# Reordering the start of a four-layer spectral kernel: x and C first, the branch later, TensorE on zeros meanwhile

## The chip, the cores and the metric
The kernel runs on one core of one Trainium2 chip. The metric is device time in microseconds (us): 1197.44 is the median of three runs (1197.13 to 1198.53). A core has TensorE (PE in the profile; PEld are its weight loads), VectorE (DVE), ScalarE (ACT), GpSimd (POOL) and SyncE (SP), which here only issues DMAs. Each engine works its own queue of instructions in order, and semaphores order the engines among each other.

## The reference, cut to what matters
Two kinds of layer alternate, A, B, A, B, on x of 2048 positions by 576 channels; each adds its result to x. The inputs of B (k, v, both kernels) are the same in both B layers.

```python
x = A_x                                        # 2048 x 576
x = x + _A_ref(_layernorm(x), dft_seq_re, dft_seq_im, dft_hid_re, dft_hid_im)
x = x + _B_ref(_layernorm(x), B_k, B_v, B_shift_k, B_ssm_k, B_ssm_D)
x = x + _A_ref(_layernorm(x), ...)             # layer 3
x = x + _B_ref(_layernorm(x), ...)             # layer 4
# _A_ref: a = x @ hid_re.T, b = x @ hid_im.T; y = seq_re @ a - seq_im @ b
# _B_ref: kv = shift_conv(k) * v; y = q * (long_conv(kv, ssm_k) + kv * ssm_D), q the normed x
```

## The kernel before
All products are in fp32r, a rounded fp32. To keep accuracy, an operand is split into a rounded part (a copy by ScalarE) and a remainder (a subtraction by VectorE); a product of two split operands takes three matmuls. `split` (L94 to L96) does this: L95 is the copy, L96 the subtraction.

**Layer 1** (`layer`, L297) multiplies the sequence matrix C with the normed x first and the hidden matrix afterwards. It goes through blocks of 512 output positions (`tb`), both matrices (`g`) and 16 rows of x (`k`, also called j); one combination is a *step*. A step is 14 matmuls: 12 on the four accumulators s (for each of four column blocks x high by C high, x high by C remainder, x remainder by C high) and 2 on rm, for the last 64 channels. Steps are counted from 0; steps 0 to 15 bring the 16 rows of x in, later steps use them again.

What a step needs: its C tile, loaded two steps ahead into the ring `craw` and split into one of three places of the ring `cs` (`load_c`); and its x row. `get_x0` (L688) loads row j+2, makes the statistics of row j and j+1 (`stats0`), scales row j and splits it (`to_x`, L190: rounding at L192, remainders at L194 and L195). For the first eight rows (ASTAT) VectorE makes the statistics (`norm_stats`, L178 to L180: 2 + 1 + 1 instructions), GpSimd the power -1/2 (L181), VectorE the bias (L187), ScalarE the scaling (L188). For the others ScalarE sums and squares (L646, L648), with one-column instructions by VectorE between (L647, L649, L672), and scales (L673). `layer` asks for rows up to XLEAD = 3 ahead.

**The branch** (`branch`, L346) computes what layer B needs of k, v and the long kernel. Its first stage, called F1 here, is a generator: each `next(br)` runs one piece. It loads rows of ssm_k (L415) and v, convolves k on VectorE (L390, L395), multiplies with v (L423), splits (L95, L96) and makes groups of six small products (`f1_products`) into banks bk, which ScalarE copies out (L448) and stores. The first piece starts the generator, which also adds a third place to `craw`. The convolution is spread over the pieces from the third feed on. The variable `used` counts pieces; after each half step the main loop runs pieces until `want`, 5 a 8 steps up to step 16, then faster, till step 42. After that follow the middle of the branch (`mid`, L509 to L531) and the hidden products of layer 1 (`hidden`, bk<-w,u), also drawn piece by piece.

**Banks.** PSUM has eight banks: four s, one rm, and three for everything else. `bank()` hands out the three in fixed turns.

**Order.** A scheduler puts the instructions of each engine into one queue, by its own estimates; `behind(i)` and `issue_after(i)` add an edge: what is issued inside stands behind i on its engine's queue. No engine waits for another by such an edge, but what stands behind a waiting instruction waits too.

**The start before**: the loading of x row 0, the first branch piece, row 0 of x, then a second piece, C of steps 0 and 1, x rows 1 and 2, two pieces, row 1, two pieces; then the steps, with `used` = 4.

Of the kernel before, what the change touches and what calls it, by code (L numbers as in the profile page):

```python
# [10 lines left out]
F32 = mybir.dt.float32  # L11
# [4 lines left out]
P = 128  # L16
# [15 lines left out]
F1_16 = 5  # L32
VW = 384
F1_END = 42
W_FROM = 41
# [30 lines left out]
def fnet_h3_kernel(ctx: ExitStack, tc: tile.TileContext, x, c_mat, w_re, w_im, k_pad, v, shift_k,  # L66
# [9 lines left out]

    banks, given = [psp.tile([P, NT], F32, tag=f"b{i}", name=f"bk{i}") for i in range(3)], [0]

    def bank():
        given[0] += 1  # L80
        return banks[(given[0] - 1) % 3]

# [77 lines left out]

    scaled = []

# [11 lines left out]
    def norm_stats(src):  # L174
        m = ring["stat"]()
        st, mv, ve, rs = m[:, :12].rearrange("p (a c) -> p a c", a=2), m[:, 12:14], m[:, 14:15], m[:, 15:16]
        for i in range(2):
            nc.vector.bn_stats(st[:, i, :], src[:, i * HD:(i + 1) * HD])  # L178
        nc.vector.bn_aggr(mv, st)
        nc.vector.tensor_scalar(ve, mv[:, 1:2], EPS, None, op0=OP.add)  # L180
        pows.append(nc.gpsimd.tensor_tensor(rs, ve, mhalf, OP.pow).ins)  # L181
        return mv, rs, m[:, 16:17]
# [26 lines left out]

    def load_c(step):  # L210
        g, tb, k = step
        raw = ring["craw"]()
        anchor.append(load_after(raw, c_mat[g, tb, k]) if anchor else nc.sync.dma_start(raw, c_mat[g, tb, k]).ins)
        c = ring["cs"]()
# [131 lines left out]
    def branch():  # L346
# [91 lines left out]
        def f1_products(j, fc, xf, at, n, so, to):  # L438
            ps = [bank()[:, :n] for _ in range(2)]
            last = seq[-1:]  # L440
            for k, (a, b) in enumerate(((0, 1), (0, 0), (1, 0))):
                for i in (1, 0):
                    half = slice(i * HP, (i + 1) * HP)
                    with behind(*last):
                        last = [mm(ps[i], fc[half, a, :], xf[b][half, at:at + n], k == 0, k == 2)]
            so = two(ring[so]())
            for i in range(2):
                stored[:] = [nc.scalar.activation(so[:, i, :], ps[i], AF.Copy).ins]  # L448
            nc.scalar.dma_start(t_d[:, j::J, to:to + n], so)
# [224 lines left out]

    XL, LN = {}, {}

    def load_x(j):
        if j < J:
            XL[j] = ring["x"]()
            nc.sync.dma_start(XL[j], x[:, j, :])  # L680

# [6 lines left out]
    def get_x0(j):  # L688
        if X[j] is None:
            if j > 0:  # L690
                load_x(j + 2)
            stats0(j)
            if j > 0:
                with behind(*stored):
                    stats0(j + 1)
# [36 lines left out]
    def done1(j, xa):  # L732
# [423 lines left out]
```

## Time and profile before
| What | us |
|---|---|
| median of three runs | 1197.44 |
| the profiled execution, its own time | 1199.58 |
| span of the profiled execution | 1197.8 |
| TensorE busy in the span | 1175.3 |
| VectorE busy | 839.2 |
| ScalarE busy | 660.5 |
| TensorE busy, first 4 us / next 4 us | 0.00 / 1.21 |
| TensorE busy, 8 to 12 us | 3.30 |
| VectorE busy, 50 to 60 us / 60 to 70 us | 8.27 / 9.56 |

Busy time counts an engine's instructions, overlaps once. The span runs from the first to the last instruction; 1.8 us of the execution lie around it. The timeline prints when an instruction or a run of equal ones started, in us from the span's start, how long it took, and in brackets how long its engine had been idle and what released it. Tiles are named output<-inputs: early and flts hold raw data, mats the split x and C, f1f and f1r the branch's rows and their split parts.

### The profile page before, as it was taken

How to read it: one execution, taken by the hardware profiler on the slowest of the kernel's cores; microseconds unless marked ns; L12 is line 12 of the kernel's file. 1: busy time of each engine (PE TensorE's matmuls, PEld its weight loads, DVE VectorE, ACT ScalarE, POOL GpSimd, SP SyncE). 2: the span in 40 equal slices, each digit the busy share in tenths (PEclk: the TensorE clock that was granted, in tenths of full speed). 3: DMA queues.
4: the chain of work that ended last, by engine and by line, in shares of the span. 5: the costliest groups of instructions: out<-in, count | busy, mean ns of one | idle time of the engine just before them, and what ended most of it. 6: DMA issues, size and time to landing. Idle time of an engine off the chain costs nothing.

```text
span 1197.8 us, 18057 instructions
## 1 busy us (share of the span) xinstructions
PE 1175.3 (98%) x6248; PEld 996.6 (83%) x6248; DVE 839.2 (70%) x1498; ACT 660.5 (55%) x1311; POOL 75.1 (6%) x116
## 2 busy tenths in 40 slices
PE   7999999999999999999999999999999999999997
PEld 5776667888888888888988898888888888789997
DVE  7899983679777677675347766865776777774764
ACT  7865555669877668775435666634444445450210
POOL 2210000000000000001101121000000000001111
PEclk9999999999999999999999999999999999999999
DMA  9869898446656667648957676872772787795621
GB/s 337 294 196 315 260 300 268 158 133 182 221 189 199 212 174 209 199 138 270 289 200 237 222 256 216 272 259 71 224 277 71 218 278 257 242 317 173 218 88 41
DMA packets 142845, 259.84 MB, mean 217 GB/s; under 512 B 15649, under 2 KB 43553, under 8 KB 142754
## 3 DMA queue, kind: packets, MB, share of 16 engines
q1 hardware_dynamic: 102674, 205.45, 52.9%
q10 hardware_dynamic: 33168, 42.63, 10.2%
q0 software_dynamic: 6912, 10.62, 3.5%
q8 instruction: 49, 0.80, 0.3%
q14 instruction: 42, 0.34, 0.1%
HBM read 191.99 MB, written 66.65 MB: 216 GB/s over the span
## 4 chain that ended last, share of the span: by engine, by line
PE 76%; ACT 2%; DVE 2%; DMA 1%; issue 1%; POOLq 0%; DVEq 0%; ACTq 0%
PE s L75 42%; PE bk L75 30%; PE rm L75 4%; ACT flts L509 1%; DMA flts<-in_c_mat 0%; ACT u L95 0%; ACT mid L509 0%; DVE u L96 0%; DVE mid L515 0%; DVE flts L529 0%; ACT mats L95 0%; DVE flts L530 0%; DMA xa<-flts 0%; DMA mid<-td 0%; DVE flts L528 0%
## 5 line engine op out<-in xcount | busy, mean ns | idle before, releaser
L75 PE MATMUL s<-mats 128*128 128x512 f32 x2088 | 541.2, 395 | 1.5 <-ACT mats L192 0.9
L75 PEld LDWEIGHTS s<-mats 128*128 128x128 f32 x2088 | 381.4, 188 | 84.1 <-issue 10.9
L96 DVE TENSOR_TENSOR mats<-flts,mats 128x512 fp32r<-128x512 f32 x206 | 140.7, 687 | 64.3 <-ACT mats L95 63.8
L95 ACT ACTIVATE mats<-flts 128x512 fp32r<-128x512 f32 x206 | 128.5, 628 | 85.4 <-PE bk L75 28.4
L75 PE MATMUL bk<-mid 128*128 128x288 f32 x768 | 135.5, 301 | 3.0 <-ACT flts L509 1.6
L75 PEld LDWEIGHTS bk<-mid 128*128 128x128 f32 x768 | 116.9, 188 | 24.1 <-ACT flts L509 7.0
L75 PE MATMUL bk<-w,u 128*128 128x288 f32 x864 | 120.6, 295 | 0.9 <-ACT w L237 0.5
L75 PEld LDWEIGHTS bk<-w,u 128*128 128x128 f32 x864 | 117.8, 188 | 3.5 <-ACT w L237 0.8
L515 DVE TENSOR_TENSOR mid<-flts,mid 128x576 fp32r<-128x576 f32 (+1 forms) x149 | 93.4, 628 | 34.3 <-ACT mid L509 30.5
L509 ACT ACTIVATE flts<-bk 128x288 f32<-128x288 f32 x160 | 62.2, 404 | 88.8 <-PE bk L75 82.4
L75 PE MATMUL rm<-mats 128*128 128x512 f32 x304 | 95.1, 391 | 0.0
L509 ACT ACTIVATE flts<-flts 64x288 f32<-64x288 f32 x192 | 85.0, 443 | 5.5
L509 ACT ACTIVATE mid<-flts 128x576 fp32r<-128x576 f32 (+1 forms) x148 | 80.4, 575 | 7.2 <-DMA flts<-td 3.1
L284 DVE TENSOR_TENSOR flts<-flts,bk 128x288 f32<-128x288 f32 x48 | 21.7, 453 | 69.9 <-PE bk L75 69.9
L448 ACT ACTIVATE flts<-bk 128x384 f32<-128x384 f32 (+1 forms) x104 | 43.1, 462 | 45.7 <-PE bk L75 45.6
L75 PE MATMUL bk<-mats 128*128 128x288 f32 (+1 forms) x376 | 67.8, 317 | 0.0
L75 PEld LDWEIGHTS rm<-mats 128*128 128x128 f32 x304 | 57.1, 188 | 12.1 <-issue 0.2
L75 PE MATMUL s<-t,mats 128*128 128x512 f32 x264 | 65.0, 390 | 0.0
L181 POOL TENSOR_TENSOR flts<-flts 128x1 f32<-128x1 f32 x35 | 28.7, 820 | 523.1 <-DVE flts L180 523.0
L75 PE MATMUL bk<-mats,t 128*128 128x288 f32 (+1 forms) x368 | 59.3, 303 | 0.0
L75 PEld LDWEIGHTS bk<-mats 128*128 128x128 f32 x376 | 55.6, 188 | 3.4
L75 PEld LDWEIGHTS s<-t,mats 128*128 128x128 f32 x264 | 49.4, 188 | 10.6 <-DVE t L96 0.4
(145 smaller groups left out, 1465.3 us busy)
## 6 DMA issues: line engine op xcount, KB each, us to landing
flts<-in_c_mat SPq DMA_DIRECT2D x148, 256.0 KB, 3.5
ph<-in_c_mat SPq DMA_DIRECT2D x54, 512.0 KB, 4.7
flts<-in_c_mat SPq DMA_DIRECT2D x30, 512.0 KB, 5.0
flts<-td SPq DMA_DIRECT2D x53, 288.0 KB, 3.1
td<-flts ACTq DMA_DIRECT2D x36, 384.0 KB, 4.6
vd<-flts ACTq DMA_DIRECT2D x64, 144.0 KB, 2.4
flts<-vd SPq DMA_DIRECT2D x32, 288.0 KB, 4.6
mid<-in_i2c POOLq DMA_DIRECT2D x32, 256.0 KB, 4.9
```

The source lines that it names most:

```text
L75: return nc.tensor.matmul(ps, lhsT, rhs, start=first, stop=last, skip_group_check=more).ins
L95: a = nc.scalar.activation(h, src, AF.Copy).ins
L96: return a, nc.vector.tensor_tensor(l, src, h.bitcast(F32), OP.subtract).ins
L181: pows.append(nc.gpsimd.tensor_tensor(rs, ve, mhalf, OP.pow).ins)
L284: added[:] = [nc.vector.tensor_tensor(r[:, cs], r[:, cs], ps[:, :HD], OP.add).ins]
L448: stored[:] = [nc.scalar.activation(so[:, i, :], ps[i], AF.Copy).ins]
L509: last_act.append(nc.scalar.activation(*args, **kw).ins)
L515: nc.vector.tensor_tensor(l, src, h.bitcast(F32), OP.subtract)
```

## The change
- The branch no longer runs at the start: `used` starts at -2, `want` is at - 2 up to step 16 (one piece a step) and as before from 16 on. Its first piece, and with it the third place of `craw`, comes in step 1. Its constants f1c all come through GpSimd's queue, since the powers are then already in the list.
- SP's queue starts with x row 0, C of step 0, x row 1, C of step 1, x row 2.
- The main code splits C of step 0 itself, its remainder behind the statistics of row 1, and runs the statistics one row ahead: row 1's behind the bias of row 0, row 2's behind C of step 1.
- `warm()` sets 512 columns of the last x row to zero and makes 18 products of them into a bank, before the first real product on TensorE's queue.
- Later x loads stand behind the last C load; the branch's pieces get further edges, behind the rounding of an x row and the last loads.
- `f1_products` and the zeros use three fixed banks in turns (`turn`); `bank()` takes a tile from the pool (tag b, three places) each time.

```diff
+WARM = 18
+    def turn():
+        given[0] += 1
+        return banks[(given[0] - 1) % 3]
     def bank():
-        given[0] += 1
-        return banks[(given[0] - 1) % 3]
+        return psp.tile([P, NT], F32, tag="b", bufs=3, name="bk")
...
         def f1_products(j, fc, xf, at, n, so, to):
-            ps = [bank()[:, :n] for _ in range(2)]
+            ps = [turn()[:, :n] for _ in range(2)]
...
             if j > 0:
-                load_x(j + 2)
+                with behind(anchor[-1]):
+                    load_x(j + 2)
             stats0(j)
             if j > 0:
-                with behind(*stored):
+                with behind(*stored, made[j - 1]):
                     stats0(j + 1)
...
+    def warm():
+        t = xs[:, J - 1, :NT]
+        nc.vector.memset(t.bitcast(F32), 0.0)
+        b = turn()
+        for i in range(WARM):
+            mm(b, t[:, :P], t, i == 0, i == WARM - 1)
...
     load_x(0)
-    next(br)
-    get_x0(0)
-    with tc.issue_after(biased[0]):
-        next(br)
-        with behind(*parted, scaled[0]):
-            load_c((0, 0, 0))
-        load_x(1)
-        with behind(rounded[0]):
-            load_c((0, 0, 1))
-        load_x(2)
-    used = 4
-    first_lo = parted[1]
-    next(br)
-    next(br)
-    with behind(first_lo):
-        get_x0(1)
-    next(br)
-    next(br)
+    raws = []
+    for i in range(2):
+        with behind(loaded[-1]):
+            raws.append(raw_step((0, 0, i)))
+        with behind(anchor[-1]):
+            load_x(i + 1)
+    warm()
+    stats0(0)
+    first = ring["cs"]()
+    CT[0, 0, 0] = first[:, :NT], first[:, NT:]
+    nc.scalar.activation(first[:, :NT], raws[0], AF.Copy)
+    next(LN[0][1], 0)
+    with behind(biased[0]):
+        stats0(1)
+    with behind(varied[1]):
+        low = nc.vector.tensor_tensor(first[:, NT:], raws[0], first[:, :NT].bitcast(F32), OP.subtract).ins
+        X[0] = to_x(LN[0][0], 0)
+    with behind(made[0]):
+        next(LN[1][1], 0)
+    with behind(biased[1], rounded[0]):
+        load_c((0, 0, 1), raws[1])
+    with behind(halved[1]):
+        stats0(2)
+    used = -2
...
-            want = int(4 + F1_16 * at / 8 if at <= 16 else at16 + (68 - at16) * (at - 16) / (F1_END - 16))
-            with behind(made[min(n + 2, J - 1)], *evac):
+            want = int((16 + 2 * F1_16 - 10) * at / 16 - 2 if at <= 16 else at16 + (68 - at16) * (at - 16) / (F1_END - 16))
+            with behind(made[min(n + 2, J - 1)], *evac, *rounded[min(n, 4) + 1:min(n, 4) + 2],
+                        *(loaded[-1:] + anchor[-1:] if n < J else [])):
```

More of the change, by code (lines that the diff above doesn't have):

```diff
@@ L75, in mm, with bank @@
         return nc.tensor.matmul(ps, lhsT, rhs, start=first, stop=last, skip_group_check=more).ins
-    banks, given = [psp.tile([P, NT], F32, tag=f"b{i}", name=f"bk{i}") for i in range(3)], [0]
-    def bank():
+    banks, given = [psp.tile([P, NT], F32, tag=f"b{i}", name=f"bf{i}") for i in range(3)], [0]
+    def turn():
         given[0] += 1
         return banks[(given[0] - 1) % 3]
+    def bank():
+        return psp.tile([P, NT], F32, tag="b", bufs=3, name="bk")
     acc4 = [psp.tile([P, NT], F32, tag=f"s{i}", name=f"s{i}") for i in range(4)]
@@ L159, in fnet_h3_kernel @@
     anchor, made, rounded, pows, biased, halved, added, evac, parted, stored = [], [], [], [], [], [], [], [], [], []
-    scaled = []
+    scaled, varied = [], []
     def load_after(dst, src):
@@ L179, in norm_stats @@
         nc.vector.bn_aggr(mv, st)
-        nc.vector.tensor_scalar(ve, mv[:, 1:2], EPS, None, op0=OP.add)
+        varied.append(nc.vector.tensor_scalar(ve, mv[:, 1:2], EPS, None, op0=OP.add).ins)
         pows.append(nc.gpsimd.tensor_tensor(rs, ve, mhalf, OP.pow).ins)
@@ L208, in fnet_h3_kernel, with raw_step @@
     CT = {}
-    def load_c(step):
+    def raw_step(step):
         g, tb, k = step
@@ L213, in load_c @@
         anchor.append(load_after(raw, c_mat[g, tb, k]) if anchor else nc.sync.dma_start(raw, c_mat[g, tb, k]).ins)
+        return raw
+    def load_c(step, raw=None):
+        raw = raw_step(step) if raw is None else raw
         c = ring["cs"]()
@@ L673, in normed_x @@
         nc.scalar.activation(y, src, AF.Identity, bias=nb, scale=rs)
-    XL, LN = {}, {}
+    XL, LN, loaded = {}, {}, []
     def load_x(j):
@@ L679, in load_x @@
             XL[j] = ring["x"]()
-            nc.sync.dma_start(XL[j], x[:, j, :])
+            loaded.append(nc.sync.dma_start(XL[j], x[:, j, :]).ins)
     def stats0(j):
```

## Prediction
> **What bounds the kernel now.** I read the busy line of the page first, then the windows, then the timeline of the first 100 us engine by engine. In the windows the columns are the stretch, its length, and the busy time of each engine with its number of instructions; then clock, DMA share, GB/s.
>
> ```profile
> PE 1175.3 (98%) x6248; PEld 996.6 (83%) x6248; DVE 839.2 (70%) x1498; ACT 660.5 (55%) x1311; POOL 75.1 (6%) x116
> ...
> 12.00:16.00 4.00, 4.00 (x11) 3.09 (x11) 4.00 (x17) 3.17 (x6) 2.17 (x4) 1.00 1.03 375
> ...
> 80.00:90.00 10.00, 9.82 (x52) 7.12 (x51) 10.00 (x12) 5.45 (x13) 1.05 (x2) 1.00 0.83 247
> ...
> 70.00:1180.00 1110.00, 1103.46 (x5898) 939.94 (x5897) 774.97 (x1347) 604.26 (x1199) 55.59 (x89) 1.00 0.67 215
> ```
>
> TensorE is busy 98% of the span; from 70 to 1180 us it idles 6.5 us (1110 - 1103.46). So over the whole kernel TensorE sets the time, and idle time at its start is lost. But between 80 and 90 us VectorE has not a tenth free either: there two engines bound one stage, and that decides this change.
>
> The start of the kernel now (start, length, engine, line, operation, tiles, count, idle time before):
>
> ```profile
> 0.81 0.06 DVE L171 MEMSET flts<- 128x1 f32 x1 [0.81 <-PEq L1148]
> ...
> 3.69 0.82 DVE L178 BATCH_NORM_STATS2 flts<-early 128x6 f32<-128x288 f32 x2 [2.82 <-DMA early<-in_x]
> ...
> 5.86 0.87 ACT L188 ACTIVATE early<-early,flts 128x576 f32<-128x576 f32 x1 [0.27 <-DVE flts L187]
> ...
> 6.64 1.09 PE L75 MATMUL bk<-f1r 64*128 64x288 f32 x6 [6.64 <-DVE f1r L96]
> ...
> 7.15 0.67 ACT L192 ACTIVATE mats<-early 128x576 fp32r<-128x576 f32 x1
> ...
> 7.88 1.56 PE L75 MATMUL s<-mats 128*128 128x512 f32 x2 [0.15 <-ACT mats L192]
> ...
> 10.14 1.09 PE L75 MATMUL bk<-f1r 64*128 64x288 f32 x6 [0.70 <-ACT flts L448]
> ...
> 11.15 4.56 PE L75 MATMUL s<-mats 128*128 128x512 f32 x10
> ...
> 15.55 0.63 PE L75 MATMUL rm<-mats 128*128 128x512 f32 x2
> ...
> 18.77 0.62 PE L75 MATMUL rm<-mats 128*128 128x512 f32 x2
> ...
> 21.95 0.61 PE L75 MATMUL rm<-mats 128*128 128x512 f32 x2
> ...
> 25.98 0.62 PE L75 MATMUL rm<-mats 128*128 128x512 f32 x2
> ```
>
> A step of layer 1 is 14 products and ends with the two on rm. The ends stand at 15.55, 18.77, 21.95: a step costs 3.18 us, 0.227 a product. From 21.95 to 25.98 one branch group (six products) lies between: it costs 0.85. The ten products from 11.15 to 15.55 take 0.44 each, twice as long, though the window from 12 to 16 shows a granted clock of 1.00: TensorE is slow until about 15.4. Step 1 thus begins at 16.0, with one step and two branch groups done.
>
> **The change at the start.** x and C come first. The first row of x keeps its place at the head of SP's queue, so its statistics start at 3.69 as before, and scaling (L188) at 5.86. The C copy that ScalarE ran between scaling and rounding is now done earlier, so rounding starts at 5.86 + 0.87 = 6.75 and ends at 7.4; the first product starts at 7.5 (before: 7.88). VectorE then makes the row's remainder (0.14 + 0.68), to 8.4; four products can run before it, ten after it: 8.4 + 10 x 0.23 = 10.7, if TensorE is fast by then. Step 1 starts at 10.7 instead of 16.0: 5.3 us earlier, less two branch groups that are still to do (2 x 0.85): TensorE is **3.6 us** ahead.
>
> The zeros. The memset follows 0.81 on VectorE, which then waits for x anyway; it costs between 0.1 and the 0.6 of a full-width operation on 512 columns, so TensorE starts on zeros at 1.0 to 1.6; I take 1.5. Slow, 18 products take 18 x 0.44 = 7.9 us, to 9.4; if the clock turns after the 5.3 us that it took here (10.14 to 15.4), at 6.8, they end at 1.5 + 5.3 + 6 x 0.23 = 8.2. Step 0 then runs 14 x 0.23 = 3.2 from there: 11.4 instead of 10.7. Ends: 0 and +4.8 (zeros and step 0 all slow: 9.4 + 14 x 0.44 = 15.5 instead of 10.7); I take a delay of **0.4**, between the case in which zeros end at 7.5 and the 8.2.
>
> [...]
>
> Loads: C of step 2 now waits until VectorE has consumed C of step 0, because the ring has two places until the branch starts, and x rows 3 and 4 queue behind it on SP.
>
> ```profile
> flts<-in_c_mat SPq DMA_DIRECT2D x148, 256.0 KB, 3.5
> ```
>
> Issued at 7.7, it lands by 11.2 (3.5 us), and step 2 needs it at 13.9. C of step 4 shares a place with that of step 3; freed at 15.7, landed at 19.2, needed at 20.2 less 0.5 for its copy. These waits fit, with under 1 us of slack: cost nothing, at most 1. The branch starts in step 1 and then runs one piece a step instead of 5/8; it has caught up at step 16. The same branch work is done, later.
>
> **The change in steps 5 to 21.** I counted instructions in the changed kernel's order. ScalarE's durations, start to start, where it waits for nothing:
>
> ```profile
> 25.65 0.68 ACT L646 ACTIVATE early<-early 128x576 f32<-128x576 f32 x1
> ...
> 26.40 0.63 ACT L95 ACTIVATE mats<-flts 128x512 fp32r<-128x512 f32 x1
> 26.94 0.67 ACT L192 ACTIVATE mats<-early 128x576 fp32r<-128x576 f32 x1
> 27.51 0.85 ACT L188 ACTIVATE early<-early,flts 128x576 f32<-128x576 f32 x1
> 28.27 0.76 ACT L648 ACTIVATE early<-early,flts 128x576 f32<-128x576 f32 x1
> ...
> 29.03 0.67 ACT L192 ACTIVATE mats<-early 128x576 fp32r<-128x576 f32 x1
> 29.61 0.68 ACT L448 ACTIVATE flts<-bk 128x288 f32<-128x288 f32 x2
> 30.18 0.68 ACT L646 ACTIVATE early<-early 128x576 f32<-128x576 f32 x1
> ```
>
> So a sum costs 0.75, a C copy 0.54, a rounding 0.57, a scaling 0.76, a square 0.76, a pair of branch copies 0.57. The copy of C step 6 waits for the end of step 3 (three cs places), at 10.7 + 3 x 3.18 = 20.2. From it to the rounding of x row 11 ScalarE has 5 C copies, 7 roundings, 6 scalings, 4 sums, 5 squares, 2 branch splits (0.58) and 3 pairs: 2.7 + 4.0 + 4.6 + 3.0 + 3.8 + 1.2 + 1.7 = 21.0 us. Row 11 is rounded at **41.2** and its remainder made at 42.0. VectorE follows ScalarE and idles: in this stretch its queue holds the sums' one-column pieces, six remainders and C copies, but no convolution, because the branch has not come so far.
>
> VectorE's durations now, from its first convolution piece (31.46) to C copy 18 (L96 at 79.14):
>
> ```profile
> 31.46 1.35 DVE L390 TENSOR_TENSOR f1f<-f1f 128x1152 f32<-128x1152 f32 x1
> ...
> 44.16 0.22 DVE L194 TENSOR_TENSOR mats<-early,mats 128x64 fp32r<-128x64 f32 x1
> ...
> 44.90 1.34 DVE L390 TENSOR_TENSOR f1f<-f1f 128x1152 f32<-128x1152 f32 x1
> 46.17 0.68 DVE L96 TENSOR_TENSOR mats<-flts,mats 128x512 fp32r<-128x512 f32 x1
> 46.77 1.34 DVE L395 TENSOR_TENSOR f1f<-f1f 128x1152 f32<-128x1152 f32 x1
> ...
> 65.14 0.75 DVE L96 TENSOR_TENSOR f1r<-f1f,f1r 128x576 fp32r<-128x576 f32 x1
> 65.81 1.35 DVE L390 TENSOR_TENSOR f1f<-f1f 128x1152 f32<-128x1152 f32 x1
> ...
> 70.89 2.47 DVE L96 TENSOR_TENSOR u<-s,u 128x512 fp32r<-128x512 f32 x4
> ...
> 75.26 0.74 DVE L423 TENSOR_TENSOR f1f<-f1f,flts 128x576 f32<-128x576 f32 x1
> ...
> 79.14 0.68 DVE L96 TENSOR_TENSOR mats<-flts,mats 128x512 fp32r<-128x512 f32 x1
> ```
>
> Now the convolution begins at 31.5; in the changed order its first piece stands behind row 11, at 42. A remainder is 0.74 (44.16 to 44.90), a convolution piece 1.27, a C copy 0.60, a branch piece 0.67, the u group 4.37. Between the remainder of row 11 and C copy 18 the changed order has 16 convolution pieces (20.3), 7 C copies (4.2), 4 remainders (3.0), 7 branch pieces (4.7), the u group (4.4) and 9 one-column pieces (0.7): 37.3 us without a gap. 42.0 + 37.3 = 79.3, plus 0.2 for two short waits: C copy 18 starts at **79.5**, against 79.14 now. Up to that copy VectorE does the same work in both kernels but for the memset; what it did between waits at 20 to 40 us it now does after 42.
>
> So TensorE, 3.6 us ahead through step 12, must wait: first in steps 13 and 14, where row 13 and C copy 14 come about 1 and 1.5 us late behind convolution pieces, then in step 18, for copy 18. Two waits of before show that this stage already hangs on the other engines:
>
> ```profile
> 56.83 1.20 PE L75 MATMUL s<-mats 128*128 128x512 f32 x4 [0.77 <-ACT mats L192]
> ...
> 95.61 0.69 ACT L95 ACTIVATE f1r<-flts 128x576 fp32r<-128x576 f32 x1 [4.18 <-DMA flts<-in_ssm_k]
> ...
> 97.10 0.80 PE L75 MATMUL bk<-f1r 64*128 64x384 f32 x6 [0.71 <-ACT flts L448]
> ```
>
> The first goes away in the new order, where row 12 is ready a step early; the last stays: there a branch load waits for its place, which VectorE frees, ScalarE waits for the load, and TensorE for ScalarE. From copy 18 to step 21 VectorE's order is unchanged, so that wait moves with VectorE.
>
> **Sum.** End = VectorE's shift at copy 18: 79.5 - 79.1 = +0.4, plus the zeros' delay of 0.4, which shifts the end of step 3 and all that hangs on it: **+0.8**. On the profiled 1199.58 (span 1197.8 and 1.8 around it) that gives 1200.4. The median of the runs is 1197.44, 2.1 lower; there I forecast **1198.2**: no change that counts. About 0.2%, 2.4 us, is what a measurement of this kernel can tell from no change.
>
> **Later stages.** Banks from the pool keep three places and three turns. Around 210 to 260 us the new order runs nine middle products together between the hidden products, where single ones were spread before.
>
> ```profile
> PE bk L75 <- ACT flts L509: 1.6, 5, 0.5
> ...
> PE bk L75 <- DVE flts L284: 0.8, 1, 0.8
> ```
>
> These are the waits that it could remove or double: -2.4 to +2.4; I take 0, since count and turns are equal.
>
> **Rivals.**
> 1. *The gain stays.* VectorE reaches copy 18 by about 76, because its work after row 11 waits less or ScalarE gets to row 11 sooner. For it: TensorE bounds the rest of the kernel. Against it: 37.3 us of work without a gap would have to shrink by 3. Then -3.6, 1193.8; with the wait of step 12 (0.77) gone too, -4.4, 1193.0. Chance 0.16.
> 2. *Slower: the zeros do not turn the clock in time.* Place: step 0. All that ends step 3 later delays ScalarE's copy 6 and the queue behind it, one for one, on top of +0.4. From a delay of 2.0 it counts: the clock turning only after 9 us. [...] For it: ten products of before ran slow after TensorE had been at work since 6.64. This is also the case that the change does not do what it says. Chance 0.18, two thirds of it over the bound.
> 3. *The pool's banks* move the hidden stage by up to 2.4 either way around 1198.2: 1195.8 to 1200.6. Chance 0.12.
> Forecast: 0.54.
>
> **How the numbers follow.** Slower by over 0.2%: 0.12 from rival 2, 0.03 from 3, 0.07 from the forecast if loads or waits of 1 to 2 us break VectorE's queue: 0.22. Faster: 0.16 + 0.02 + 0.02 = 0.20. Same: 0.58. The range goes from 1193.5, which takes in rival 1 at 3.6, to 1201.0, the zeros at 3.2.
>
> **What would show it.** TensorE's first real product near 7.5 and step 3 ending near 20.2 (the start is right); x row 11 rounded near 41; VectorE without a gap from 42 to 80, C copy 18 near 79.5 to 80.5; waits of TensorE for VectorE in steps 13, 14 and 18, some 4 to 5 us in all. I am wrong if VectorE reaches copy 18 before 77, if the products of step 0 are 0.44 apart, or if the times differ after 100 us.

## The result, and the profile after

The changed kernel takes **1207.39 us** (median of five runs, 1206.49 to 1209.32), the kernel before in the same comparison 1198.20 (1197.13 to 1199.17). The ratio is 1.0077 with a 95% interval of 1.0065 to 1.0089: 9.2 us slower, where I forecast 1198.2 with a range up to 1201.0. The profiled execution of the changed kernel took 1206.49 with a span of 1204.7; against the profiled one of before that is 6.9 us.

First the page and the windows of the changed kernel, as they were read for the kernel before.

```profile
PE 1180.3 (98%) x6266; PEld 999.7 (83%) x6266; DVE 841.7 (70%) x1499; ACT 660.5 (55%) x1310; POOL 76.6 (6%) x117
...
PEclk9989999999999999999999999999999999999999
```

```profile
70.00:80.00 10.00, 5.86 (x27) 4.06 (x24) 10.00 (x14) 4.67 (x10) 0.53 (x1) 0.83 0.76 234
80.00:90.00 10.00, 10.00 (x43) 7.40 (x42) 9.30 (x12) 4.59 (x10) 0.53 (x1) 0.83 0.61 183
70.00:1180.00 1110.00, 1099.73 (x5854) 935.66 (x5851) 778.68 (x1347) 606.71 (x1205) 55.10 (x89) 1.00 0.67 216
```

The busy shares of the page have hardly moved, since 6.0 us of zeros now count as TensorE's work. The windows tell more: from 70 to 80 us TensorE is busy 5.86 of 10, beside a VectorE without a gap, and the granted clock is 0.83 there and in the next window. Set beside each other, the products of the two traces stand like this: the changed kernel is 4.8 us ahead at the end of step 0, 4.5 ahead at the first product of step 11 (three branch groups are still to do), 2.3 behind at the last of step 15 and 8.6 behind at the last of step 16, where both have done the same groups. Later it is 8.4 behind at step 20, 7.6 at 290 us and 8.6 at 573 us. So the loss is made between 48 and 84 us. TensorE's timeline there, after four rows of the start:

```profile
1.49 5.99 PE L76 MATMUL bf<-mats 128*128 128x512 f32 x18 [1.49 <-DVE mats L754]
7.47 3.41 PE L76 MATMUL s<-mats 128*128 128x512 f32 x12
10.72 0.61 PE L76 MATMUL rm<-mats 128*128 128x512 f32 x2
...
20.28 0.62 PE L76 MATMUL rm<-mats 128*128 128x512 f32 x2
...
52.49 0.67 PE L76 MATMUL bf<-f1r 64*128 64x288 f32 x6 [0.96 <-ACT flts L456]
...
56.62 0.66 PE L76 MATMUL bf<-f1r 64*128 64x288 f32 x6 [1.89 <-ACT flts L456]
57.22 2.09 PE L76 MATMUL s<-mats 128*128 128x512 f32 x8
...
74.89 0.66 PE L76 MATMUL bf<-f1r 64*128 64x288 f32 x6 [0.87 <-DVE f1r L100]
78.63 5.24 PE L76 MATMUL s<-mats 128*128 128x512 f32 x12 [3.08 <-DVE u L100]
```

The start is as forecast (first product 7.47, step 0's last products at 10.72, step 3's at 20.28). The last row carries the largest piece of the loss: TensorE waits 3.08 us for u, and the twelve products behind that wait take 5.24 us. In the kernel before, the same twelve wait for nothing and take 3.02, so this is another 2.2 us:

```profile
72.22 3.02 PE L75 MATMUL s<-mats 128*128 128x512 f32 x12
```

The way from 4.5 us ahead to 8.6 behind, 13.1 us, is thus 8.5 us of waits against 0.8 in the kernel before, 2.2 us of slow products, and for most of the remaining 3.2 the three branch groups (0.85 each by the prediction's rows). ScalarE in that stretch:

```profile
21.16 0.69 ACT L654 ACTIVATE early<-early 128x576 f32<-128x576 f32 x1 [0.98 <-DMA early<-in_x]
...
22.60 0.61 ACT L99 ACTIVATE mats<-flts 128x512 fp32r<-128x512 f32 x1
...
43.55 0.67 ACT L196 ACTIVATE mats<-early 128x576 fp32r<-128x576 f32 x1
...
44.77 0.61 ACTq L457 DMA_DIRECT2D td<-flts  x1
...
52.02 0.41 ACT L456 ACTIVATE flts<-bf 128x288 f32<-128x288 f32 x1 [2.53 <-DMA td<-flts]
...
55.86 0.71 ACT L456 ACTIVATE flts<-bf 128x288 f32<-128x288 f32 x2 [1.94 <-DMA td<-flts]
```

The row at 22.60 is the copy of C step 6, that at 43.55 the rounding of x row 11. At 52.02 a branch copy waits for its place in the ring of four: the store that holds it was issued at 44.77, long after its own copies (the second of them ended at 33.1), and everything behind it in ScalarE's queue waits too. VectorE, to C copy 18:

```profile
44.70 0.68 DVE L199 TENSOR_TENSOR mats<-early,mats 128x512 fp32r<-128x512 f32 x1
45.30 1.35 DVE L398 TENSOR_TENSOR f1f<-f1f 128x1152 f32<-128x1152 f32 x1
...
53.29 0.69 DVE L100 TENSOR_TENSOR mats<-flts,mats 128x512 fp32r<-128x512 f32 x1 [0.64 <-ACT mats L99]
...
57.12 0.69 DVE L100 TENSOR_TENSOR mats<-flts,mats 128x512 fp32r<-128x512 f32 x1 [1.68 <-ACT mats L99]
...
77.88 2.49 DVE L100 TENSOR_TENSOR u<-s,u 128x512 fp32r<-128x512 f32 x4
...
86.14 0.68 DVE L100 TENSOR_TENSOR mats<-flts,mats 128x512 fp32r<-128x512 f32 x1
```

Row 11's remainder ends at 45.3 (forecast 42.0), the first convolution piece follows, and C copy 18 starts at **86.14** (forecast 79.5, before 79.14).

### The profile page after: what moved, and what is told of

It is laid out like the page before. It is cut to its first block, busy times and chain, and to the rows that moved or that the text cites. A ratio compares the mean times of both kernels' runs of the same rounds, so it can differ in the third digit from the quotient of the medians.

```text
span 1204.7 us, 18094 instructions
## 1 busy us (share of the span) xinstructions
PE 1180.3 (98%) x6266; PEld 999.7 (83%) x6266; DVE 841.7 (70%) x1499; ACT 660.5 (55%) x1310; POOL 76.6 (6%) x117
## 3 DMA queue, kind: packets, MB, share of 16 engines
q10 hardware_dynamic: 33168, 42.63, 10.1%
## 4 chain that ended last, share of the span: by engine, by line
PE 72%; ACT 4%; DVE 2%; DMA 1%; issue 1%; ACTq 0%; POOL 0%; DVEq 0%; SPq 0%; POOLq 0%
PE s L76 40%; PE bk L76 29%; PE rm L76 4%; ACT flts L517 2%; ACT mid L517 1%; DVE mid L523 0%; ACT mats L99 0%; DMA flts<-in_c_mat 0%; DMA flts<-td 0%; ACT u L99 0%; DMA wd<-w 0%; DVE u L100 0%; DMA vd<-flts 0%; DVE flts L538 0%; DVE flts L537 0%
## 5 line engine op out<-in xcount | busy, mean ns | idle before, releaser
L99 ACT ACTIVATE mats<-flts 128x512 fp32r<-128x512 f32 x205 | 127.6, 628 | 82.2 <-PE bk L76 33.8
L76 PE MATMUL bk<-mid 128*128 128x288 f32 x768 | 132.3, 299 | 4.4 <-ACT flts L517 3.6
L456 ACT ACTIVATE flts<-bf 128x384 f32<-128x384 f32 (+1 forms) x104 | 43.2, 463 | 48.4 <-PE bf L76 41.3
```

Of the source, the lines that this page charges most:

```text
L76: return nc.tensor.matmul(ps, lhsT, rhs, start=first, stop=last, skip_group_check=more).ins
L99: a = nc.scalar.activation(h, src, AF.Copy).ins
```

## The experiments

A diff with L99, L457 and the like is against the changed kernel, unless it says "before". Theories came and went; each is said where it first counts. The table has the four numbers that all runs were read by: the time, the ratio to the kernel before, C copy 18 on VectorE, and the place of step 20's products on TensorE against the kernel before (both from the trace). Each of the last two columns is one execution. The changed kernel and e3, and the kernel before and e4, run the same instructions in the same order up to 100 us, and still differ there by 1.0 to 1.8 us, so a difference under 2 us in these columns says little.

| Run | us | ratio, 95% interval | copy 18 | step 20 |
|---|---|---|---|---|
| before | 1198.2 | | 79.1 | 0 |
| changed | 1207.4 | 1.0077 (1.0065 to 1.0089) | 86.1 | +8.4 |
| e1 stores early | 1208.7 | 1.0088 (1.0074 to 1.0102) | 85.6 | +7.9 |
| e2 early pace | 1208.1 | 1.0082 (1.0069 to 1.0096) | 86.9 | +6.9 |
| e3 fixed banks | 1205.4 | 1.0066 (1.0053 to 1.0079) | 84.9 | +6.6 |
| e4 before, pool's banks | 1195.1 | 0.9976 (0.9967 to 0.9985) | 78.1 | -1.0 |
| e5 convolution early | 1204.1 | 1.0051 (1.0036 to 1.0067) | 85.9 | +6.0 |
| e6 cover | 1204.0 | 1.0051 (1.0038 to 1.0064) | 87.5 | +8.3 |
| e7 pace, stores, f1c | 1207.8 | 1.0079 (1.0065 to 1.0092) | 86.2 | +6.3 |
| e8 no zeros | 1206.2 | 1.0064 (1.0049 to 1.0079) | 86.1 | +8.9 |
| e9 preload | 1211.3 | 1.0108 (1.0094 to 1.0121) | 90.0 | +11.4 |
| e10 preload, convolution | 1205.4 | 1.0055 (1.0043 to 1.0068) | 82.9 | +3.0 |
| e11 the same, stores | 1203.3 | 1.0041 (1.0028 to 1.0054) | 84.5 | +4.6 |
| e12 before, more traffic | 1197.7 | 0.9994 (0.9985 to 1.0003) | 77.7 | -2.1 |
| e13 before, late branch | 1200.9 | 1.0023 (1.0013 to 1.0033) | 82.0 | +3.7 |
| e14 before, zeros | 1197.0 | 0.9990 (0.9981 to 0.9999) | 77.1 | -2.7 |
| e15 before, zeros, pool | 1198.5 | 0.9998 (0.9989 to 1.0007) | 77.5 | -2.3 |
| e16 e15, convolution | 1198.6 | 0.9998 (0.9989 to 1.0007) | 79.0 | -0.9 |
| e17 less traffic | 1207.8 | 1.0078 (1.0063 to 1.0093) | 86.8 | +8.3 |
| e18 before, less traffic | 1199.9 | 1.0012 (1.0004 to 1.0021) | 79.1 | +0.3 |

In every run the last two columns move together, within 2 us: where VectorE stands at copy 18 is where TensorE stands at step 20. That one follows the other is read from TensorE's last wait (for u, which VectorE makes), not from the table.

**e1: the stores right behind their copies.**

```diff
-            nc.scalar.dma_start(t_d[:, j::J, to:to + n], so)
+            stored[:] = [nc.scalar.dma_start(t_d[:, j::J, to:to + n], so).ins]
```

> The changed kernel with one edge more: what ScalarE issues behind a branch group's copies stands behind the group's store as well, so that the store goes out right after its copies (in the changed kernel the first store was issued at 44.8 us, the copies that it stores had ended at 33). Theory A (late stores): the copies at 52.0 and 55.9 waited 2.5 and 1.9 us for places held by stores not yet landed; ScalarE, VectorE (0.6 + 1.7 us idle) and at last TensorE (3.1 us for u) are late from this, and the long wait drops the granted clock, so that 12 products take 0.44 instead of 0.23 us. Then the waits for td vanish, C copy 18 on VectorE starts 2.3 us sooner (83.8), the wait for u falls under 1.5 us, the clock stays at 1.00 from 75 to 85 us, and the time falls by 4 to 6 us, to 1201.5 to 1203.5. Theory B (late convolution): VectorE has 37 us of work behind row 11 in any case and row 11 is 3.3 us late; without the stores' wait only 2.3 us of 8.6 come back and the clock falls all the same: 1204.5 to 1206. If neither, 1206.5 to 1208.5.

1208.7: theory A failed. The first store went out at 33.7 instead of 44.8 us, and no copy waits for a store. But ScalarE's queue stops elsewhere, at a C copy whose load has not come (first fence, ScalarE), and TensorE's wait for u is longer, not shorter (second fence):

```profile
48.76 0.63 ACT L99 ACTIVATE mats<-flts 128x512 fp32r<-128x512 f32 x1 [2.70 <-DMA flts<-in_c_mat]
```

```profile
78.05 5.28 PE L76 MATMUL s<-mats 128*128 128x512 f32 x12 [3.67 <-DVE u L100]
```

**e2: the branch at its old pace, from step 1.**

```diff
-            want = int((16 + 2 * F1_16 - 10) * at / 16 - 2 if at <= 16
+            want = int(min(2 * at - 2, 4 + F1_16 * at / 8) if at <= 16
```

> The changed kernel with the branch drawn early: two pieces a step until it has the pace of the kernel before (5 in 8 steps, from 4), so that the convolution starts on VectorE behind row 7 instead of row 11. Theory B (late convolution): VectorE's idle time between 20 and 42 us is filled, C copy 18 starts by 79 us or sooner, TensorE waits under 1 us for u, and the start's gain is kept: 1194 to 1198. Theory A (late stores): the stores still stand far behind their copies in ScalarE's queue, its copies go on waiting for them, and 3 us or more of the loss stay: 1201 to 1205.

1208.1: neither. The convolution started at 35.2 instead of 45.3, and copy 18 was no earlier. Two new waits for DMA took the time: TensorE's for f1c, with slow products behind it, and ScalarE's for a store.

```profile
25.04 0.80 PE L76 MATMUL bf<-f1r 64*128 64x288 f32 x6 [4.06 <-DMA f1r<-in_f1c]
25.77 3.74 PE L76 MATMUL s<-mats 128*128 128x512 f32 x9
```

```profile
54.76 0.41 ACT L456 ACTIVATE flts<-bf 128x288 f32<-128x288 f32 x1 [4.29 <-DMA td<-flts]
```

**e3 and e4: the banks by themselves.** e3 gives the changed kernel the fixed banks back everywhere; e4 gives the kernel before the pool's banks and nothing else.

```diff
     def bank():
-        return psp.tile([P, NT], F32, tag="b", bufs=3, name="bk")
+        return turn()
```

> The changed kernel with the three fixed banks in turns everywhere, as in the kernel before; all else as changed. Theories A and B: the loss lies before 85 us, where both kernels have fixed banks, so the time stays within 1.5 us of the changed kernel: 1206 to 1209. Rival (the pool's banks cost): 1204 or less.

> The kernel before with nothing but the pool's banks behind the first stage of the branch. Theories A and B: within 1.5 us of the kernel before, 1196.7 to 1199.7. Rival (the pool's banks cost): 1200.5 or more.

e3 came out at 1205.4, 2.0 below the changed kernel, with intervals that overlap. Its trace does not put these 2.0 on the pool's banks. The first product into such a bank comes at 218 us in the changed kernel, and at step 20 e3 is already 1.8 better, with the same instructions in the same order. The same wait of 3.08 us stands there, but the products behind it take less:

```profile
77.39 4.61 PE L76 MATMUL s<-mats 128*128 128x512 f32 x12 [3.08 <-DVE u L100]
```

Behind step 20 the two hardly part: at 955 us the changed kernel is 8.6 behind the kernel before (8.4 at step 20), e3 6.9 (6.6). e4 came out at 1195.1, 2.9 us faster than the kernel before in the same comparison: alone the banks gain. In e4's trace TensorE's distance to the kernel before is -0.7 at 204 us, -3.1 at 266 and -3.6 later, so 2.4 of the gain lie where the branch's middle and the hidden products mix. Why the banks gain there, and not in the changed kernel, is not settled.

**e5: the convolution from the first feed on.**

```diff
-                if later and n > 2:
+                if later and n > 0:
```

> The changed kernel with the convolution spread from the first feed on instead of the third; pieces and pace of the branch stay. In VectorE's queue the first convolution piece moves from behind row 11 to behind row 7. Theory B (VectorE's work between row 11 and C copy 18 is what is late): VectorE's idle time before 42 us takes three to five pieces of 1.27 us, C copy 18 starts by 82 to 83 us instead of 86.1, the wait for u falls under 1 us and the clock stays: 1200 to 1204. Theory C (each cure moves the wait: the loads and stores that come earlier meet full DMA engines and another engine waits over 2.5 us): the time stays at 1205 to 1209 and the trace shows a new long wait of TensorE with half-speed products behind it.

1204.1: 3.3 us back, within theory B's range, but not by its way (the intervals of e5 and of the changed kernel just touch). The convolution started at 32.2, yet copy 18 at 85.9: what VectorE won before 45 us it lost behind ScalarE, which waited for a store (first fence). What is better is the last wait of TensorE, 1.84 instead of 3.08, with no slow products behind it (second fence); against that, a wait of 2.09 at 40.4 has slow products behind it in this trace (3.69 us for eight).

```profile
60.31 0.71 ACT L456 ACTIVATE flts<-bf 128x288 f32<-128x288 f32 x2 [3.52 <-DMA td<-flts]
```

```profile
78.42 3.04 PE L76 MATMUL s<-mats 128*128 128x512 f32 x12 [1.84 <-DVE u L100]
```

**e6: products of no use in the wait.**

```diff
+            if whole and n == J - 1:
+                with behind(seq[-1]):
+                    b = turn()
+                    for i in range(13):
+                        mm(b, xs[:, 0, :P], xs[:, 0, :NT], i == 0, i == 12)
```

> The changed kernel with 13 products of no use (a row of x by itself, into a free bank) between step 15 and step 16, where TensorE waits 0.9 and 3.1 us and the 12 products behind run at 0.44 us. The wait itself stays, since VectorE sets its end. If the clock falls because of the idle stretch, the twelve products take 0.23 us each again, and 2 to 3 us come back: 1204 to 1205.5. Rival (the clock falls for the idle time of the whole stretch from 50 us, or for another reason): products at 0.44 all the same, 1206.5 to 1209.

1204.0, 3.4 less than the changed kernel, with intervals just apart. TensorE's timeline:

```profile
75.23 1.29 PE L76 MATMUL bf<-mats 128*128 128x512 f32 x5
76.46 0.67 PE L76 MATMUL bf<-f1r 64*128 64x288 f32 x6
77.05 2.13 PE L76 MATMUL bf<-mats 128*128 128x512 f32 x8
79.97 3.00 PE L76 MATMUL s<-mats 128*128 128x512 f32 x12 [0.79 <-DVE u L100]
```

Twelve products in 3.00 instead of 5.24, at a granted clock of 1.00 from 70 to 90 us instead of 0.83: here the half speed came of the idle stretch, and work without use in it took it away. (In the profiled execution an earlier wait, 2.95 us at 58, slowed TensorE as well, with a clock of 0.83 from 50 to 70, which is why its step 20 stands no better than the changed kernel's. The runs as a whole are 3.4 faster.)

**e7: e2, with its two DMA waits attacked**: the store edge of e1, and f1c issued behind earlier powers.

```diff
-                        load_fr(fcs[j], f1c[j])
+                        with tc.issue_after(pows[min(1 + len(fcs), len(pows) - 1)]):
+                            nc.gpsimd.dma_start(fcs[j], f1c[j])
```

> The changed kernel with the early pace of e2, the store edge of e1, and the branch's constants f1c issued by GpSimd from its third power on, one behind each, instead of behind the latest power. In e2 TensorE waited 4.1 us for f1c and 2.8 us for a row that stood behind a copy waiting for a store, and both waits halved the clock. Theory B with both waits taken away: VectorE's work is spread, C copy 18 by 80 us, no wait of TensorE over 2 us before 100 us: 1194 to 1198. Theory C: another long wait comes instead, 1200 or more.

1207.8: nothing gained; theory C holds here. The wait for f1c is gone, and ScalarE waits 2.1 us for ssm_k at 34 and 4.1 for a store at 54.

**e8: no zeros** (`WARM = 0`).

> The changed kernel without the zeros. Step 0 and part of step 1 run at 0.44 us a product, so TensorE is some 3 us later at step 4. If the loss between steps 12 and 16 is set by VectorE and ScalarE (theories A to C), which run ahead of TensorE only by what their own queues allow, most of these 3 us vanish in TensorE's waits: 1206.5 to 1209. By my forecast (the end of step 3 starts ScalarE's queue and shifts the end one for one): 1209.5 to 1211.

1206.2: not slower. TensorE's rows (first fence) and VectorE's copy 18 (second):

```profile
7.54 5.66 PE L76 MATMUL s<-mats 128*128 128x512 f32 x12 [7.54 <-ACT mats L196]
13.04 0.63 PE L76 MATMUL rm<-mats 128*128 128x512 f32 x2
...
78.58 5.49 PE L76 MATMUL s<-mats 128*128 128x512 f32 x12 [3.08 <-DVE u L100]
```

```profile
86.08 0.68 DVE L100 TENSOR_TENSOR mats<-flts,mats 128x512 fp32r<-128x512 f32 x1
```

Step 0 ends 2.3 us later than with zeros, and at 78.6 the same wait of 3.08 ends at the same time, with copy 18 within 0.1 us. In the changed kernel these 2.3 us of TensorE's lead are worth nothing.

**e9 to e11: the branch's loads early.** The trace shows 10.1 MB moved by 30 us before, and 7.0 after, so a theory D: the DMA engines are what binds. e9 starts the branch before step 0 (one load, the third place of `craw`) and loads five pieces in steps 0 to 4 (`PRE_AT` is 0); e10 adds the edit of e5, e11 that of e1 too.

```diff
+        early_loads.extend([lambda: load_w4(1), lambda: load_k(1), lambda: load_w4(2), lambda: load_k(2), lambda: load_k(3)])
+        yield
...
+    with behind(loaded[-1]):
+        next(br)
     used = -2
...
+        if whole and PRE_AT <= n < PRE_AT + 5:
+            with behind(anchor[-1], loaded[-1]):
+                early_loads.pop(0)()
```

> The changed kernel with the branch started before step 0 (one of its loads, the third place of craw) and its first 2.9 MB loaded a piece a step in steps 0 to 4: both halves of shift_k and three pieces of k_pad. Its computing pieces keep their pace. Theory D (the DMA engines): the kernel before keeps them busy from 5 to 45 us and has moved 10.1 MB by 30 us, the changed kernel 7.0 MB; the missing 3.1 MB are 8 us of them at 390 GB/s, and whatever needs data between 40 and 60 us waits: stores, C, x, ssm_k, f1c. Then over 8.5 MB are moved by 30 us, ScalarE's waits for DMA between 40 and 60 us fall from 4.5 to under 1.5 us, and the time falls to 1202 to 1205. Theory B (VectorE alone): its queue still has the convolution behind row 11, so 1206 to 1208.5.

> As e9, and the convolution spread from the first feed on as in e5. Theories B and D together: VectorE has data and work before 42 us; its busy time by 80 us rises from 62 to 65 us or more (the kernel before: 67), TensorE has no wait over 2 us between 10 and 100 us: 1197 to 1201. Theory B alone: as e5, 1203 to 1205.5.

> As e10, with the store edge of e1. Where ScalarE's copies still wait for stores in e10, this takes their wait away: 1196 to 1200 by theories B and D; the same as e10 if the stores have landed in time there.

e9: 1211.3, the worst of all. By 30 us 7.9 MB were moved, more than the 7.0 but less than the 8.5 that theory D asked for, so this is no clean test of it. With the third place a C copy stands ahead of row 0's scaling in ScalarE's queue, and its remainder ahead of row 0's bias on VectorE; that copy waited 2.8 us for its load, so step 0's lead was gone (step 0 only 0.5 ahead of the kernel before); a store still cost ScalarE 3.7 us. e10 and e11, 1205.4 and 1203.3, are better than the changed kernel by 2 and 4 us (e10's interval overlaps its, e11's does not). They too lose the lead at the start (1.9 and 0.6 us left), and it does not hurt: e11 has the fewest long waits of ScalarE and the lowest time of the kernels with the new start, though not apart from e5 and e6. None reaches the kernel before.

**e12: more traffic in the kernel before.** In steps 1 to 8 SyncE also copies an x row to a scratch tensor that nothing reads.

```diff
+        if whole and 1 <= n < 9:
+            with behind(anchor[-1]):
+                nc.sync.dma_start(junk_d[n - 1], x[:, n - 1, :])
```

> The kernel before with 2.36 MB more to move and nothing that waits for it: in each of the steps 1 to 8, SyncE issues a copy of an x row from memory to a scratch tensor (8 x 288 KB). Theory D: the DMA engines are full between 5 and 45 us, so these 2.36 MB are 6 us of them at 390 GB/s, loads land later, and 3 to 7 us are lost: 1201 to 1205. Theory B: DMA is not what binds, 1197.5 to 1199.5.

1197.7: theory D failed. The kernel before (first row: windows of before, second: of the changed kernel) has its DMA engines full from 5 to 45 us, the changed kernel a fifth less. Yet 2.1 MB more by 70 us cost the kernel before nothing. They did not fit in beside the full stretch: from 5 to 45 us e12 moved 351 GB/s against 361, and from 45 to 70 us 311 against 212. So some of the kernel's own transfers came later, and no time was lost by it.

```profile
5.00:45.00 40.00, 37.51 (x164) 28.35 (x166) 33.16 (x91) 34.07 (x69) 9.43 (x15) 1.00 1.02 361
```

```profile
5.00:45.00 40.00, 39.17 (x179) 29.89 (x178) 28.77 (x90) 34.31 (x66) 11.59 (x17) 1.00 0.81 271
```

The third and fourth busy times are what counts: by 45 us VectorE has worked 33.2 us of these 40 before and 28.8 after, ScalarE 34 in both.

**e13: the late branch alone, in the kernel before.**

```diff
-            want = int(4 + F1_16 * at / 8 if at <= 16
+            want = int((16 + 2 * F1_16 - 10) * at / 16 - 2 if at <= 16
```

> The kernel before with nothing but the changed kernel's pace of the branch: its start and four first pieces stay, then no piece until step 7 and one a step up to 16. In VectorE's queue the first convolution piece stands behind row 11, as in the changed kernel, instead of row 7. Theory B (VectorE is idle before the late branch and cannot make it up by copy 18; the new start has no part in it): copy 18 at 84 to 87 us, 1203 to 1207. Theory E (it takes the new order of loads and rows at the start as well): 1197 to 1200.

1200.9, between the ranges of the two theories: slower by 2.5 us, with an interval clear of 1. With nothing of the new start, the convolution begins at 44.3 behind row 11, and copy 18 is 2.9 us late (first fence, VectorE). TensorE then waits for u, and the products behind are slow (second fence): the pattern of the changed kernel at about a quarter of its price.

```profile
44.27 1.35 DVE L390 TENSOR_TENSOR f1f<-f1f 128x1152 f32<-128x1152 f32 x1
...
82.04 0.68 DVE L96 TENSOR_TENSOR mats<-flts,mats 128x512 fp32r<-128x512 f32 x1
```

```profile
74.54 4.62 PE L75 MATMUL s<-mats 128*128 128x512 f32 x12 [2.31 <-DVE u L96]
```

No copy waits for a store here: two groups of the branch are done before step 1, and their stores went out at 10.9 and 36.3 us.

**e14 to e16: what is good of the change, in the kernel before.** e14 adds `warm()` as in the changed kernel, before row 0; e15 adds the edit of e4; e16 also `if later and n > 1`.

> The kernel before with nothing but the memset and 18 products of zeros ahead of its first products. The ten products of step 0 that took 0.44 us take 0.23, so TensorE is 2 to 3 us ahead from step 1. Theory B: VectorE sets copy 18, which it reaches at the same time, and TensorE gives the lead back in waits: 1197 to 1199.5. Rival (TensorE sets the end of this stage as long as the branch is early): 1195 to 1196.5.

> The kernel before with the zeros and the pool's banks (e4 and e14 together, the branch early). If e4's gain of 2.9 us comes from the stage after 200 us, it adds to whatever the zeros bring: theory B 1194.5 to 1196.5, rival 1192 to 1194.

> e15 with the convolution spread from the second feed on, so that VectorE takes it up behind row 5 instead of row 7. Theory B (VectorE's idle time before 45 us is what limits TensorE's lead): copy 18 one to two us earlier than in e15, 1193 to 1195. If VectorE's queue has no idle time left to win there, the same as e15 within 1 us.

e14: 1197.0, a gain of 1.5 us with an upper bound just under 1; copy 18 came 2 us earlier and TensorE was still 2.7 ahead at step 20, so here its earlier start is passed on, against theory B. e15 and e16: 1198.5 and 1198.6, no gain, and e15 outside both ranges. TensorE's lead in e15 goes from 2.5 us at 371 to 0.2 at 738, which it does not in e14 (2.9 to 2.6); e15 has the pool's banks beyond e14, which were worth 2.9 us in e4. e16's earlier convolution did not bring copy 18 forward (79.0). The fastest of all is e4, with nothing but the pool's banks: it beats both kernels, by 0.24% and 1.0%.

**e17 and e18: less traffic.** In the changed kernel (e17) and in the kernel before (e18), C of steps 6 to 15 is loaded in its first 128 of 512 columns only; the others keep what an earlier step left there.

```diff
-        anchor.append(load_after(raw, c_mat[g, tb, k]) if anchor else
+        w = P if g == tb == 0 and 6 <= k < J else NT
+        anchor.append(load_after(raw[:, :w], c_mat[g, tb, k][:, :w]) if anchor else
```

> The changed kernel, with C of steps 6 to 15 loaded in its first 128 of 512 columns only (the others keep what an earlier step left there): 10 x 192 KB = 1.9 MB less between 16 and 55 us, with the same instructions and waits in nearly the same order. Theory F (in the changed kernel loads and stores of the branch, of x and of C meet after 30 us, and their latency is what ScalarE and VectorE wait for): stores land in under 5 us, the wait of 4.5 us for them goes, and 2.5 to 5 us are gained: 1202.5 to 1205. Theory G (the order in the queues, with the late convolution, and not the traffic): 1206 to 1208.5.

> The kernel before with the same columns of C left out. Both theories: its stage is not short of data, 1196.5 to 1199. If it gains over 2 us as well, traffic binds both kernels, and e17 says nothing about the change.

1207.8 and 1199.9: theory F failed, theory G stands (e18 is 1.1 us slower than the kernel before, not faster). With 1.4 MB less moved by 50 us, the stores landed 6.1 us after their issue instead of 7.1 (DMA lines of the two kernels, 25 to 60 us), ScalarE's two waits for them were 4.4 instead of 4.5 us, and TensorE's last wait was 3.08 again.

```profile
td<-flts ACTq DMA_DIRECT2D x4, 288.0 KB, 7.1
```

```profile
td<-flts ACTq DMA_DIRECT2D x4, 288.0 KB, 6.1
```

## Why the prediction was wrong

- **The start**: right. First product at 7.47 (7.5), step 3 ended at 20.7 (20.2 + 0.4). The zeros cost no delay, since the first product starts at 7.54 without them (e8): in the trace the clock turns at 4.92, 3.4 us after they began, and from the ninth zero on they start 0.23 apart.
- **"Loads: these waits fit, cost nothing, at most 1"**: wrong, by its consequence. ScalarE waited 0.98 us for x row 8, within the bound, but in its queue the sum of row 8 and a scaling (1.44 together) stand ahead of the copy of C step 6, so that this copy, from which I counted, came at 22.60 instead of 20.2: 2.4 late.
- **ScalarE's queue, 21.0 us from that copy to row 11**: 20.95 (22.60 to 43.55), but by luck: the trace has six roundings in it where I counted seven (0.57), and a wait of 0.56 for ssm_k that I did not have. Row 11's remainder ended at 45.3 instead of 42.0, 3.3 late: the 2.4, and 0.9 because VectorE waited 0.66 for a power ahead of it.
- **"37.3 us without a gap"**: this is the step that failed. The work was counted right. It took 40.8 us (45.30 to 86.14), because VectorE waited 2.3 us for C copies and 0.9 us for powers. The C copies stood on ScalarE behind branch copies, which waited 4.5 us for stores. I named the copies and never asked for the ring of four places that they write into, nor where in ScalarE's queue its stores stand. So copy 18 came at 79.5 + 3.3 (row 11) + 3.3 (40.8 instead of 37.5) = 86.1. Such a break of VectorE's queue had a chance of 0.07 in the prediction, with waits of 1 to 2 us.
- **TensorE's waits, "some 4 to 5 us, giving back all of its 3.6"**: the mechanism was right (it waits for VectorE in these steps), the size wrong: 8.5 us of waits between 50 and 79, and half speed behind the last one, 2.2 us more for twelve products. A wait that slows what follows was in my rival 2, at the start; I did not ask for it in the middle. e6 shows a price: 3.4 us less in the runs when the wait is filled with work.
- **The moved branch**: "the same branch work is done, later" was costed at nothing but its place on VectorE. e13 shows that the lateness alone costs 2.5 us; the chain that I worked out gives it (row 11, then packed work, then copy 18), with an end 2.9 late instead of 0.4.
- **The pool's banks**: "I take 0" held in the changed kernel, as far as e3 tells (from step 20 to 955 us the changed kernel loses 0.2 us, e3 with its fixed banks 0.3). In the kernel before they gained 2.9 (e4), 2.4 of it in the stage that the bounds of -2.4 to +2.4 were made for.
- **Rival 2 (slower)** had the right side and the wrong place: without zeros the time is the same (e8).

What makes 9.2: the late branch alone costs 2.5 (e13). Half speed has a share in it (4.62 us for twelve products in e13) and in the rest: the mean granted clock was 0.993 to 0.996 in the five runs of the changed kernel, and 0.997 to 0.999 in those of the kernel before (0.996 once). A difference of 0.003 over 1205 us is an estimate of some 4 us of clock, of which a part falls on time in which TensorE waits anyway. These shares overlap, so they are not a sum. The other 6 to 7 us beyond e13 come with the new start, and no single edge of it owns them. Stores (e1), f1c (e2 against e7) and traffic (e17) were taken away one by one; in e1, e2, e7 and e9 ScalarE's in-order queue stopped for 2 to 4 us at other transfers, and in e17 at the same stores. That the branch's early pieces, two groups of them done before step 1, are what kept this queue free is my reading of e13 beside the changed kernel. It was not shown by a run that has the new start and these pieces in their old place, and a larger ring than four places was not tried.

## What to carry to other kernels

An engine's early start is worth only what the next engine behind it can follow: look up who sets the end of the stage (here VectorE's copy 18) and ask of every edit whether that instruction comes earlier. When work is moved later, follow its buffers as well as its instructions: the ring that it writes into, the stores that free it, and where those stores stand in an in-order queue. Ask of a wait on TensorE what it does to the products behind it: here twelve products took 5.24 us behind a wait of 3.08 and, in e13, 4.62 behind one of 2.31, against 3.02 without a wait, but 3.06 behind one of 2.80 in e10; in e6, products of no use in the wait took that cost away (3.00). And one profiled execution is one sample: two kernels with the same instructions up to 100 us stood 1.8 us apart there.

## What the runs showed of the hardware

Half speed after idle time: in the traces of the two kernels the granted clock changes at times that lie whole multiples of 3.41 us apart. In the changed kernel it turns up at 4.92, falls at 76.60 and rises at 83.43 us: 71.68 us are 21 such stretches and 6.83 are two. In the kernel before it turns up at 15.51 and falls at 1193.11: 1177.60 us are 345. The clock records of these traces begin with the first turn; ahead of it the windows print 1.00 although products are 0.43 apart, as from 12 to 15 us in the kernel before. The rows are three stretches of the changed kernel, one of e13 and two of e10; the first busy time is TensorE's, and behind the busy times stands the clock.

```profile
73.19:76.60 3.41, 1.49 (x10) 0.80 (x8) 3.41 (x5) 1.72 (x4) 0.00 (x0) 1.00 0.89 240
76.60:80.02 3.42, 1.39 (x3) 1.16 (x4) 3.42 (x6) 0.59 (x1) 0.00 (x0) 0.50 0.74 269
80.02:83.43 3.41, 3.41 (x9) 2.64 (x8) 2.71 (x5) 2.26 (x5) 0.00 (x0) 0.50 0.04 5
```

```profile
71.87:75.28 3.41, 1.09 (x9) 0.74 (x6) 3.41 (x6) 0.71 (x2) 0.00 (x0) 1.00 0.26 92
```

```profile
5.91:9.32 3.41, 2.00 (x9) 1.32 (x7) 1.09 (x3) 0.87 (x2) 0.00 (x0) 1.00 1.03 388
9.32:12.73 3.41, 2.01 (x9) 1.65 (x10) 3.34 (x11) 2.83 (x5) 0.93 (x1) 1.00 0.68 230
```

Of these stretches at full clock, two were followed by one at half clock: that with TensorE busy 1.49 of 3.41 in the changed kernel, and that with 1.09 of 3.41 in e13 (4.62 us for the twelve products behind it, and a mean clock of 0.66 from 75 to 80 us). The two with 2.00 and 2.01 of 3.41 in e10 were not (3.06 for twelve, 1.00 from 10 to 15 us), nor was one with 1.87 of 3.42 in the changed kernel (first row below, at 1.00 behind it as well). So 2.31 us of wait inside one stretch came with half clock (e13), while 2.80 us across two did not (e10): that the place of a wait on these stretches decides is my reading of these rows. In the changed kernel the clock stayed low for two stretches, the first with TensorE busy 1.39 of 3.42, the second 3.41 of 3.41. In e3, behind the same wait of 3.08, it was low for less time: its mean from 40 to 100 us was 0.97, against 0.94 in the changed kernel.

```profile
52.71:56.13 3.42, 1.87 (x11) 1.07 (x9) 2.15 (x4) 1.48 (x5) 0.00 (x0) 1.00 1.03 374
56.13:59.54 3.41, 2.91 (x15) 2.04 (x15) 2.42 (x4) 3.41 (x9) 0.31 (x1) 1.00 0.60 220
```

Eight waits of 2.95 us (e6) to 4.06 (e2) had a lower clock behind them: in the changed kernel, e1, e2, e6, e8, e9 and e17 the lowest window of 5 or 10 us there has a mean of 0.55 to 0.83, and the eighth is e3's. Of shorter ones, 2.02 (e11), 2.09 (e5), 2.31 (e13), 2.36 (e9) and 2.81 us (e2) had one too, with means of 0.66 to 0.85; 2.35 (e3: 2.11 us for the eight products behind it) and 2.80 us (e10) had none. The 18 zeros needed 5.99 us in the changed kernel, where the second to the eighth started 0.43 apart and, once the clock had turned 3.4 us after they began, the later ones 0.23 apart. By the next row they needed 6.97 in e14; at 0.2 us between the two spacings these 0.98 us are about five more products at the slow one, by which I estimate a turn some 2 us later there.

```profile
1.49 6.97 PE L75 MATMUL bk<-mats 128*128 128x512 f32 x18 [1.49 <-DVE mats L745]
```

DMA engines at a share of 1.02 from 5 to 45 us moved no more when 2.1 MB were added (e12: 351 against 361 GB/s); the surplus went to the next 25 us, and the kernel lost no time. A full share did not mean here that the kernel waits for a transfer.
